# Two-part masked attention feeding a gated FFN on one core: products of zeros on TensorE in the opening, another order of opening loads and x pieces, a second batch masked by TensorE, and softmax pairs seven slots apart

## The chip, the core and the metric

The program runs on one core of a Trainium2 chip. The metric is the device time of one launch in microseconds, taken as the median of several runs. TensorE (PE in the profile, its weight loads PEld) does the matrix products, VectorE (DVE), ScalarE (ACT) and GpSimd (POOL) do elementwise work, and SyncE (SP) issues the DMAs. TensorE's clock has two levels, 1.2 and 2.4 GHz; the profile shows the granted one as a share of full speed.

## The reference

```python
# q, k, v: 8 batches, 8 heads, 576 positions, 64 wide
scores = scale * np.matmul(q, k.transpose(0, 1, 3, 2))
mask_local = (rel >= 0) & (rel < 32)                              # heads 0..3
mask_strided = (rel >= 0) & (pos[None, :] % 32 == pos[:, None] % 32)  # heads 4..7
scores = np.where(masks[None], scores, -1000000000.0)
attn = softmax(scores); attn_out = np.matmul(attn, v)
x = attn_out as (4608 tokens, 512)
h = x @ w_in                                                      # 512 -> 2048
g = h * (1.0 / (1.0 + np.exp(-1.702 * h)))
return g @ w_out                                                  # 2048 -> 512
```

## The kernel before

**Three stages.** The opening does the attention of batch 0 and prepares the first two weight blocks. Then eight passes, one for each batch, multiply x by w_in; each pass has eight weight blocks (`FP`), and during a pass the attention of the next batch is done beside the products. The results go to DRAM (`hid`). The last stage, from about 539 us, reads them back, applies the gate and multiplies by w_out; the change does not touch it.

**Products.** Each block of weights against one batch of x is done as seven products of half-size pieces (`product(n, k)`, k from 0 to 6, with sums and differences of quarters on both sides) instead of eight. Every number is split into a high part and a rest, so a product is six matmuls of 128x128 by 128x288. `combine(n, k)` takes the results out of PSUM: ACT copies for k = 0 and 2, DVE adds for the others.

**Slots.** The passes are written as a list of slots, one product each on average: block n begins at slot 7n and issues product k at slot 7n + 2k, so that two blocks interleave; a pass is 56 slots. In each slot first come the product and its combine, then whatever `side(slot, ...)` has put there, in the order of registration. All engines keep this program order until the last stage, so an instruction that waits holds everything behind it on its engine.

**Pairs.** The attention of a batch is six pairs (`PAIRS`), three local ones (96 queries in three windows) and three strided ones (128 rows). A pair goes through `scores` (TensorE, into the two banks `s_banks`), `masked` (DVE), `maxima` (DVE), `below` (POOL, subtracts the maximum), `exps` (ACT), `totals` (DVE), `scaled` (POOL), `turn` (four transposes on TensorE into `s_banks[0]`, an ACT copy) and `values` (TensorE into both `s_banks`, copied by ACT into the quarters of x, `xr`). For the six pairs of batch 0 (`p < PAIRS`, line 210) TensorE adds the mask itself: a product of the mask with an identity starts each bank and the scores are added to it; then `masked` takes the maximum out of PSUM and subtracts it, on DVE, and `maxima` and `below` aren't called. In a pass for batch b the pairs of batch b + 1 stand eight slots apart (seven in the first pass), line 558, with offsets 0, 1, 2, 3, 5, 6 for the six softmax steps and 11 and 14 for `turn` and `values`.

**x pieces.** From the quarters `11`, `12`, `21`, `22` four sums are made (`x_sum(1)`, `x_sum(2)` on DVE, `x_sum(3)`, `x_sum(4)` on POOL), in place where they can be. `x_high(k)` (ACT) and `x_low(k)` (DVE) split piece k into `xv[k]`, which product k reads. Since `values` of the next batch overwrites the quarters, its copies wait until `x_low` has read them. Lines 550 to 555 place these steps around the border between two passes (`at` is the first slot of the pass).

**Weights.** For each block of w_in, `w_scale` and `w_low` (ACT), `w_join` (DVE) put the numbers together from words, `w_sums` (POOL, four subtractions) makes the sums, `w_high` (ACT) and `w_rest` (DVE) split them, three quarters first (`sums` False) and four sums after (`sums` True). Blocks 0 and 1 are made in the opening, 2 to 7 in the first pass by `weigh` (line 567).

**The opening.** Lines 474 to 486 issue the loads; the loop at 489 runs nine steps, each with the scores of pair i, the transposes of pair i - 2, the values of pair i - 3, and the softmax steps; lines 527 to 539 prepare x pieces and block 1 before the first pass starts. Arena tiles hold most buffers and are reused: `mid[0]`, which the change also uses, is first written by a combine.

Of the kernel before, what the change touches and what calls it, by code (L numbers as in the profile page):

```python
# [30 lines left out]
FP = DFF // (2 * P)  # L31
PAIRS = 6
QL, KL = 96, 128
WL = 64
# [34 lines left out]
def attn_ffn(ctx, tc, qk, vs, weights, masks, ident, out):  # L69
# [84 lines left out]
    warm = const.tile([P, 1], F32, name="warm")  # L154
    vector.memset(warm, 0.0)
    scalar.activation(warm, warm, AF.Exp)
    for x in prs:
# [47 lines left out]
    def scores(p, banks):  # L205
# [3 lines left out]
        t = qks[p]  # L209
        onto = p < PAIRS  # L210
        if onto:
# [38 lines left out]
    def masked(p, banks):  # L250
        nq, nk, mask, pr, heads, srcs, (nmax, _, _) = parts_of(p, banks)
        if p < PAIRS:
            by = nmax[:nq].rearrange("p (i j) -> p i j", j=2)
            for j in range(2):
                vector.tensor_reduce(
                    out=by[:, :, j], in_=srcs[j], axis=AX.X, op=ALU.max, negate=True
                )
            for j in range(2):
                vector.tensor_tensor(
                    out=pr[:nq, :, j, :nk], in0=srcs[j], in1=over(by[:, :, j], 4, nk), op=ALU.add  # L260
                )
            return
# [16 lines left out]
    def exps(p, banks):  # L279
        heads = parts_of(p, banks)[4]  # L280
        scalar.activation(heads, heads, AF.Exp, scale=SCALE if p < PAIRS else 1.0)

# [18 lines left out]

    def values(p, banks):

# [21 lines left out]
        for u in range(U):  # L325
            src = banks[u][:, : 2 * n0].rearrange("p (g n) -> p g n", g=2)
            if kind == "l":
                h, o = divmod(c + u, 3)
                scalar.copy(out=x[("11", "21")[h]][:, :, o * QL : (o + 1) * QL], in_=src)
                continue  # L330
            n, r0, half = RES[c], R0[c + u], NPOS // 2
            src = src.rearrange("p g (r t) -> p g t r", r=n)
            for k, h in enumerate(("12", "22")):
                o = x[h].rearrange("p g (t r) -> p g t r", r=STRIDE)[:, :, :, r0 : r0 + n]
                scalar.copy(out=o, in_=src[:, :, k * half : (k + 1) * half])

# [15 lines left out]
    def x_sum(k):  # L352
# [3 lines left out]
        elif k == 2:  # L356
            vector.tensor_tensor(out=xr["11"], in0=xr["s1"], in1=xr["11"], op=ALU.subtract)
        elif k == 3:
# [27 lines left out]

    def w_sums(raw):
        f = raw.bitcast(F32)
        b11, b21, b22, b12 = (f[:, q, :, 1] for q in range(4))
        t1, t2, t3, t4 = (f[:, q, :, 0] for q in range(4))  # L390
        for o, x, y in ((t1, b12, b11), (t2, b22, t1), (t3, b22, b12), (t4, b21, t2)):
            gpsimd.tensor_tensor(out=o, in0=x, in1=y, op=ALU.subtract)
# [15 lines left out]

    def w_rest(i, raw, sums):
        src, hi, lo = w_part(i, raw, sums)  # L410
        vector.tensor_tensor(out=lo, in0=src, in1=hi.bitcast(F32), op=ALU.subtract)

# [66 lines left out]
    load_qk(2)  # L479
    load_v(1)  # L480
    load_w(0)
    for i in range(3, n0):
        load_qk(i)
        load_v(i - 1)
    load_v(n0 - 1)
    load_w(1)
    all_banks = [m_banks[i][x] for x in ("mx", "my", "mz") for i in range(2)]

    for i in range(n0 + 3):
        if i < n0:  # L490
            ss = all_banks[2 * (i % 2) : 2 * (i % 2) + 2]
# [3 lines left out]
        if 2 <= i <= n0 + 1:  # L495
            turn(i - 2, all_banks[4 + i % 2])
        if i >= 3:
            values(i - 3, s_banks)
            if i < 5:
                load_v(n0 + i - 3)  # L500
# [9 lines left out]
        if i == 4:  # L510
            w_join(raws[0])
            w_sums(raws[0])
            w_high(0, raws[0], False)
        if i == 5:
            w_rest(0, raws[0], False)
            w_high(0, raws[0], True)
        if i == 6:
            x_high(0)
            x_sum(3)
            w_rest(0, raws[0], True)  # L520
            x_low(0)
            w_scale(raws[1])
            w_low(raws[1])
        if i == 7:
            w_join(raws[1])
            w_sums(raws[1])
    load_w(2)
    x_sum(1)
    x_sum(2)
    for k in range(1, 7):  # L530
        x_high(k)
        x_low(k)
        if k == 2:
            x_sum(4)
            w_high(1, raws[1], False)
            w_rest(1, raws[1], False)
        if k == 4:
            w_high(1, raws[1], True)
            w_rest(1, raws[1], True)

# [7 lines left out]
    for b in range(B):  # L548
        at = b * PASS
        if b:  # L550
            for k, t in ((1, -9), (3, -8), (2, -5), (4, -1)):
                side(at + t, x_sum, k)
            for k, t in enumerate((-7, -4, -3, -1, 1, 3, 5)):
                side(at + t, x_high, k)
                side(at + t + (k < 6), x_low, k)
        for i in range(PAIRS if b + 1 < B else 0):
            p = (b + 1) * PAIRS + i
            s, t, t2 = (at - 9 + 8 * i, 11, 14) if b else (7 * i, 10, 12)
            side(s, scores, p, s_banks)
            side(s, load_qk, p + 2)  # L560
            for f, d in ((masked, 0), (maxima, 1), (below, 2), (exps, 3), (totals, 5), (scaled, 6)):
                side(s + d, f, p, s_banks)
# [4 lines left out]
    def weigh(i, at, then):  # L567
# [9 lines left out]
        for t, sums in ((0, False), (2, True)):  # L577
            later(then + t, w_high, i, sums)
            later(then + t + 1, w_rest, i, sums)

# [309 lines left out]
```

## Time and profile before

| | |
|---|---|
| median of 3 runs | 906.07 us (904.57 to 906.53) |
| profiled execution | 906.79 us, its span 904.8 us |
| granted clock, mean | 0.983 |
| PE busy | 851.1 us (94%) |
| DVE, ACT, POOL busy | 575.9, 418.8, 520.2 us |

The span runs from the first to the last instruction; the other 2.0 us of the profiled execution lie around it. Busy times are unions of an engine's instructions, and a busy PE is not a PE at its peak. The rows that matter are in the section further down: rows of stretches give the stretch and its length, then for each engine the busy time and the count of instructions, the granted clock and the DMA share; rows of the timeline give start, duration, engine, what was written from what, and in brackets the idle time before and what ended it.

### The profile page before, as it was taken

Reading aid. Unit: us, or ns where it says so; the run is one execution under the profiler, and the core shown is the slowest. Engines: PE = TensorE matmul, PEld = TensorE weight load, DVE = VectorE, ACT = ScalarE, POOL = GpSimd, SP = SyncE. Lnnn points to the kernel's source line nnn. Section 1 sums busy time; section 2 is a strip of 40 time slices with the busy share of each in tenths; the row PEclk is TensorE's granted clock in tenths of the full one; section 3 lists DMA queues with packets and bytes.
Section 4 is the critical chain, followed back from the end, with each engine's and each line's share of the span. In section 5 each row is a group of like instructions: output and inputs, shape, how many; then the busy total and the mean of one; then the engine's idle time right before and its main releaser. Section 6 shows DMA issues by size and latency. Waiting matters only on the chain.

```text
span 904.8 us, 23885 instructions
## 1 busy us (share of the span) xinstructions
PE 851.1 (94%) x9756; PEld 820.8 (91%) x9756; DVE 575.9 (64%) x941; ACT 418.8 (46%) x669; POOL 520.2 (57%) x497
## 2 busy tenths in 40 slices
PE   6689989989899899899899999999999999999997
PEld 4588879979899799799799999999999999999997
DVE  5798865655855755756656776665665566655663
ACT  3666533433433433434333655645554555445650
POOL 2667433423432432434331618999989998989990
PEclk9999999989999899999899999999999999999999
DMA  9358446647565557475556885344334434444331
GB/s 357 143 184 276 149 157 207 209 160 226 171 211 190 184 197 224 158 233 194 164 165 208 254 261 169 125 136 144 125 117 145 135 117 135 133 130 140 117 117 47
DMA packets 109644, 156.42 MB, mean 173 GB/s; under 512 B 9440, under 2 KB 87520, under 8 KB 108512
## 3 DMA queue, kind: packets, MB, share of 16 engines
q1 hardware_dynamic: 109536, 154.92, 52.8%
q8 instruction: 76, 1.25, 0.6%
q14 instruction: 32, 0.26, 0.1%
HBM read 100.35 MB, written 54.53 MB: 171 GB/s over the span
## 4 chain that ended last, share of the span: by engine, by line
PE 57%; DVE 15%; DMA 11%; issue 6%; ACT 5%; POOL 4%; SPq 2%; DVEq 0%; ACTq 0%; POOLq 0%
PE my L85 19%; PE mz L85 15%; PE mx L85 14%; PE s L85 10%; DMA arena<-hid 8%; DVE xa L85 6%; DVE arena L85 4%; POOL arena L85 3%; DVE ga L85 2%; ACT xa L85 2%; DMA hid<-arena 2%; SPq L85 2%; ACT arena L85 1%; POOL raw L85 1%; DMA early<-qk 1%
## 5 line engine op out<-in xcount | busy, mean ns | idle before, releaser
L85 POOL TENSOR_TENSOR arena<-arena 128x256 f32<-128x256 f32 (+1 forms) x304 | 354.4, 1183 | 118.5 <-ACT arena L85 46.6
L85 DVE TENSOR_TENSOR xa<-arena,xa 128x576 fp32r<-128x576 f32 (+1 forms) x104 | 171.4, 1657 | 70.9 <-ACT xa L85 68.5
L85 PE MATMUL my<-xa,w 128*128 128x288 f32 x1152 | 189.6, 308 | 5.3 <-DVE arena L85 4.2
L85 ACT ACTIVATE arena<-arena 128x1024 f32<-128x1024 f32 (+2 forms) x120 | 105.0, 876 | 174.0 <-DMA arena<-hid 149.0
L85 PEld LDWEIGHTS my<-xa,w 128*128 128x128 f32 x1152 | 166.9, 197 | 9.2 <-DVE arena L85 5.3
L85 DVE TENSOR_TENSOR arena<-mz,arena 128x288 f32<-128x288 f32 (+1 forms) x182 | 78.9, 442 | 88.4 <-PE mz L85 86.4
L85 PE MATMUL mx<-xa,w 128*128 128x288 f32 x768 | 129.1, 304 | 2.6 <-ACT arena L85 2.6
L85 PE MATMUL mz<-xa,w 128*128 128x288 f32 x768 | 130.5, 307 | 0.0
L85 ACT CAST xa<-arena 128x576 fp32r<-128x576 f32 (+1 forms) x104 | 118.2, 1140 | 21.0 <-DVE arena L85 11.0
L85 DVE TENSOR_TENSOR arena<-my,arena 128x288 f32<-128x288 f32 (+1 forms) x228 | 100.2, 444 | 40.8 <-PE my L85 40.0
L85 ACT COPY arena<-mx 128x288 f32<-128x288 f32 (+1 forms) x146 | 57.5, 394 | 142.5 <-PE mx L85 118.1
L85 POOL TENSOR_TENSOR arena<-arena,rinv 96x512 f32<-96x512 f32 (+1 forms) x48 | 52.3, 1091 | 114.8 <-DVE rinv L85 103.5
L85 PEld LDWEIGHTS mx<-xa,w 128*128 128x128 f32 x768 | 110.1, 192 | 4.6 <-ACT arena L85 3.0
L85 PEld LDWEIGHTS mz<-xa,w 128*128 128x128 f32 x768 | 112.5, 196 | 1.7 <-DVE arena L85 0.4
L85 POOL TENSOR_TENSOR arena<-arena,nmax 128x432 f32<-128x432 f32 (+1 forms) x42 | 48.9, 1165 | 101.4 <-DVE nmax L85 101.0
L85 ACT COPY arena<-s 128x90 f32<-128x90 f32 (+4 forms) x186 | 51.5, 339 | 110.5 <-PE s L85 91.8
L85 PEld LDWEIGHTS s<-arena 64*64 64x64 f32 (+2 forms) x3456 | 58.8, 133 | 39.5 <-ACT arena L85 26.6
L85 PE MATMUL s<-arena 64*64 64x32 f32 (+4 forms) x3456 | 70.6, 229 | 24.2 <-ACT arena L85 24.2
L85 PE MATMUL mx<-w_out,xa 128*128 128x256 f32 x576 | 84.0, 280 | 1.8 <-DVE xa L85 1.8
L85 PE MATMUL my<-w_out,xa 128*128 128x256 f32 x576 | 83.2, 280 | 0.0
L85 PE MATMUL mz<-w_out,xa 128*128 128x256 f32 x576 | 83.1, 280 | 0.0
L85 PEld LDWEIGHTS mx<-w_out,xa 128*128 128x128 f32 x576 | 74.6, 188 | 2.4 <-DVE xa L85 2.4
(62 smaller groups left out, 1049.3 us busy)
## 6 DMA issues: line engine op xcount, KB each, us to landing
hid<-arena SPq DMA_DIRECT2D x256, 144.0 KB, 2.6
arena<-hid SPq DMA_DIRECT2D x144, 256.0 KB, 3.3
arena<-qk SPq DMA_DIRECT2D x23, 448.0 KB, 4.1
arena<-qk SPq DMA_DIRECT2D x21, 472.0 KB, 3.8
out<-arena SPq DMA_DIRECT2D x36, 256.0 KB, 2.2
arena<-vs SPq DMA_DIRECT2D x23, 384.0 KB, 3.9
raw<-w_in SPq DMA_DIRECT2D x8, 1024.0 KB, 8.0
stage<-w_out SPq DMA_DIRECT2D x16, 512.0 KB, 4.9
```

Of the source, the lines that this page charges most:

```text
L85: ins = call(*args, **kw)
```

## The change

It has five parts.

1. `fill(n, bank)` issues n bf16 products of a zeroed tile (128x128 by 128x512) into a bank of PSUM that is unused at that time. In the steps of the opening loop 9, 3, 4, 1, 1, 1, 2, 3, 3 of them come first in TensorE's order, and 4 more before the first pass. DVE zeroes the tile (`mid[0]`).
2. The loads of pair 3's q and k and pair 2's v are issued before the first block of w_in instead of behind it. In the opening, the work on block 0 is spread over other steps (two of its sums go one step later), x piece 3 is prepared inside the loop, and the pieces left over follow in the order 2, 1, 5, 4, 6. In the loop's last step DVE copies the second bank of values. `x_sum(2)` is computed from `22` and `s3`.
3. `ONTO = 12` takes the place of `PAIRS` in the mask's conditions: batch 1's pairs are masked by TensorE too, without `maxima` and `below`, and `exps`, `totals`, `scaled` follow at offsets 2, 4, 5.
4. `w_rest` of the three quarters goes from DVE to POOL for block 0 and for blocks 2 to 7.
5. From the second pass on the pairs stand seven slots apart, the first three slots before the border; `exps`, `totals`, `scaled`, `turn`, `values` move to offsets 5, 6, 7, 10, 12. `x_sum`, `x_high` and `x_low` around the border get other slots.

```diff
+ONTO = 2 * PAIRS
...
+    zeros = mid[0].bitcast(BF16)[:, :512]
+    vector.memset(mid[0], 0.0)
...
-        onto = p < PAIRS
+        onto = p < ONTO
...
-        scalar.activation(heads, heads, AF.Exp, scale=SCALE if p < PAIRS else 1.0)
+        scalar.activation(heads, heads, AF.Exp, scale=SCALE if p < ONTO else 1.0)
...
+            copy = vector.tensor_copy if shared and u else scalar.copy
...
-            vector.tensor_tensor(out=xr["11"], in0=xr["s1"], in1=xr["11"], op=ALU.subtract)
+            vector.tensor_tensor(out=xr["11"], in0=xr["22"], in1=xr["s3"], op=ALU.subtract)
...
-    def w_rest(i, raw, sums):
+    def w_rest(i, raw, sums, engine=None):
         src, hi, lo = w_part(i, raw, sums)
-        vector.tensor_tensor(out=lo, in0=src, in1=hi.bitcast(F32), op=ALU.subtract)
+        (engine or vector).tensor_tensor(out=lo, in0=src, in1=hi.bitcast(F32), op=ALU.subtract)
...
+    load_qk(3)
+    load_v(2)
     load_w(0)
-    for i in range(3, n0):
+    for i in range(4, n0):
         load_qk(i)
         load_v(i - 1)
...
+    def fill(n, bank):
+
+        for _ in range(n):
+            matmul(bank, lhsT=zeros[:, :P], rhs=zeros, start=True, stop=True)
+
+    FILL = (9, 3, 4, 1, 1, 1, 2, 3, 3)
     for i in range(n0 + 3):
+        late = all_banks[4 + i % 2]
+        fill(FILL[i], late)
...
         if i == 4:
             w_join(raws[0])
-            w_sums(raws[0])
+            w_sums(raws[0], (0, 1))
+        if i == 5:
+            w_sums(raws[0], (2, 3))
             w_high(0, raws[0], False)
-        if i == 5:
-            w_rest(0, raws[0], False)
-            w_high(0, raws[0], True)
         if i == 6:
             x_high(0)
+            x_low(0)
             x_sum(3)
+            w_high(0, raws[0], True)
             w_rest(0, raws[0], True)
-            x_low(0)
+            w_rest(0, raws[0], False, gpsimd)
+        if i == 7:
+            x_high(3)
             w_scale(raws[1])
             w_low(raws[1])
-        if i == 7:
+            x_low(3)
             w_join(raws[1])
             w_sums(raws[1])
     load_w(2)
+    fill(4, all_banks[5])
+    x_high(2)
+    x_sum(2)
+    x_low(2)
+    x_high(1)
+    x_low(1)
     x_sum(1)
-    x_sum(2)
...
+    x_sum(4)
+    x_high(5)
+    w_high(1, raws[1], False)
+    x_low(5)
+    x_high(4)
+    x_low(4)
+    w_rest(1, raws[1], False)
+    w_high(1, raws[1], True)
+    x_high(6)
+    x_low(6)
+    w_rest(1, raws[1], True)
...
         if b:
-            for k, t in ((1, -9), (3, -8), (2, -5), (4, -1)):
-                side(at + t, x_sum, k)
-            for k, t in enumerate((-7, -4, -3, -1, 1, 3, 5)):
-                side(at + t, x_high, k)
-                side(at + t + (k < 6), x_low, k)
+            first = -8 if b == 1 else -11
+            side(at + first, x_sum, 1)
+            side(at + first + 1, x_sum, 3)
+            for k in range(7):
+                t = at + 2 * k - 6 + (k == 1)
+                side(t, x_high, k)
+                side(t + 1, x_low, k)
+            side(at - 4, x_sum, 2)
+            side(at, x_sum, 4)
...
-            s, t, t2 = (at - 9 + 8 * i, 11, 14) if b else (7 * i, 10, 12)
+            s, t, t2 = (at - 3 + 7 * i, 10, 12) if b else (7 * i, 10, 12)
             side(s, scores, p, s_banks)
             side(s, load_qk, p + 2)
-            for f, d in ((masked, 0), (maxima, 1), (below, 2), (exps, 3), (totals, 5), (scaled, 6)):
+            side(s, masked, p, s_banks)
+            if p < ONTO:
+                soft = ((exps, 2), (totals, 4), (scaled, 5))
+            else:
+                soft = ((maxima, 1), (below, 2), (exps, 5), (totals, 6), (scaled, 7))
+            for f, d in soft:
                 side(s + d, f, p, s_banks)
...
-            later(then + t + 1, w_rest, i, sums)
+            later(then + t + 1, w_rest, i, sums, *([] if sums else [gpsimd]))
```

## Rows read from the trace of the kernel before

**Rows 1.** Stretches, TensorE's products of x only: length, busy (count), clock, DMA, GB/s
```profile
48.20:113.00 64.80, 49.34 (x318) 1.00 0.66 212
...
429.40:491.30 61.90, 50.37 (x337) 0.94 0.55 177
```

**Rows 2.** The same view, two of the five stretches between borders
```profile
126.10:181.20 55.10, 47.04 (x322) 1.00 0.61 197
...
378.70:434.60 55.90, 48.20 (x330) 1.00 0.65 212
```

**Rows 3.** Waits of TensorE, 112 to 500 us: total, times, longest
```profile
PE s L85 <- ACT arena L85: 21.8, 6, 4.3
```

**Rows 4.** Timeline around the third of six borders
```profile
238.40 0.96 PE L85 MATMUL mz<-xa,w 128*128 128x288 f32 x6
...
241.34 1.36 POOL L85 TENSOR_TENSOR arena<-arena,nmax 96x512 f32<-96x512 f32 x1 [1.35 <-DVE nmax L85]
...
244.70 0.67 DVE L85 TENSOR_REDUCE ssum<-arena 96x8 f32<-96x512 f32 x1
...
246.15 1.54 DVE L85 TENSOR_TENSOR xa<-arena,xa 128x576 fp32r<-128x576 f32 x1
...
247.78 0.71 ACT L85 COPY arena<-s 128x108 f32<-128x108 f32 x4 [2.98 <-DVE xa L85]
...
248.23 1.08 PE L85 MATMUL s<-arena 64*64 64x54 f32 x32 [2.55 <-ACT arena L85]
...
249.24 1.81 PE L85 MATMUL mz<-xa,w 128*128 128x288 f32 x6
```

**Rows 5.** Stretches around two borders: PE, PEld, DVE, ACT, POOL, clock, DMA, GB/s
```profile
246.00:254.00 8.00, 5.77 (x58) 5.55 (x59) 4.61 (x9) 1.34 (x6) 1.96 (x2) 0.79 0.67 205
308.00:318.00 10.00, 6.16 (x56) 6.04 (x57) 6.00 (x14) 1.28 (x6) 4.48 (x6) 0.66 0.39 119
```

**Rows 6.** Timeline of the opening, TensorE alone
```profile
4.33 0.66 PE L85 MATMUL mx<-masks_sb 96*96 96x256 bf16 x2 [4.33 <-DMA masks_sb<-masks]
...
14.13 1.12 PE L85 MATMUL my<-early 64*64 64x54 f32 x32 [1.49 <-DMA early<-qk]
...
17.92 1.12 PE L85 MATMUL mx<-early 64*64 64x54 f32 x32
...
27.92 1.11 PE L85 MATMUL mz<-ident_sb,arena 128*128 128x128 f32 x4 [2.14 <-POOL arena L85]
...
34.24 1.33 PE L85 MATMUL s<-arena,early 54*64 54x54 f32 x32 [1.87 <-ACT arena L85]
...
48.20 1.81 PE L85 MATMUL my<-xa,w 128*128 128x288 f32 x6 [2.20 <-DVE arena L85]
```

**Rows 7.** Stretches of the opening, columns as in rows 5
```profile
14.00:26.00 12.00, 11.43 (x256) 9.32 (x256) 8.49 (x23) 6.56 (x13) 5.50 (x6) 1.00 1.03 401
...
36.10:48.20 12.10, 6.23 (x50) 4.76 (x48) 11.17 (x15) 7.80 (x12) 5.21 (x5) 1.00 0.36 127
```

**Rows 8.** Timeline of one weight block in the first pass
```profile
66.04 1.21 DVE L85 SCALAR_TENSOR_TENSOR raw<-raw 128x1024 uint32<-128x1024 uint32 x1
...
67.33 3.91 POOL L85 TENSOR_TENSOR raw<-raw 128x256 f32<-128x256 f32 x4 [3.03 <-DVE raw L85]
...
68.81 1.14 DVE L85 TENSOR_TENSOR w<-raw,w 128x768 fp32r<-128x768 f32 x1
...
72.08 1.04 POOL L85 TENSOR_TENSOR arena<-arena,nmax 96x512 f32<-96x512 f32 x1
...
72.43 1.77 DVE L85 TENSOR_TENSOR w<-raw,w 128x1024 fp32r<-128x1024 f32 x1 [0.86 <-ACT w L85]
...
74.86 1.21 DVE L85 SCALAR_TENSOR_TENSOR raw<-raw 128x1024 uint32<-128x1024 uint32 x1
```

**Rows 9.** Timeline late in the first pass: a transpose's wait, a POOL subtraction
```profile
98.72 0.55 PE L85 MATMUL s<-ident_sb,arena 96*128 96x96 f32 x4 [1.25 <-POOL arena L85]
...
103.16 1.44 POOL L85 TENSOR_TENSOR arena<-arena 128x576 f32<-128x576 f32 x1 [4.50 <-DVE arena L85]
```

More of the change, by code (lines that the diff above doesn't have):

```diff
@@ L251, in masked @@
         nq, nk, mask, pr, heads, srcs, (nmax, _, _) = parts_of(p, banks)
-        if p < PAIRS:
+        if p < ONTO:
             by = nmax[:nq].rearrange("p (i j) -> p i j", j=2)
@@ L300, in turn, with values @@
         scalar.copy(out=pts[p % 2][:, : 4 * nq], in_=bank[:, : 4 * nq])
-    def values(p, banks):
+    def values(p, banks, shared=False):
         kind, b, c = pairs[p]
@@ L326, in values @@
             src = banks[u][:, : 2 * n0].rearrange("p (g n) -> p g n", g=2)
+            copy = vector.tensor_copy if shared and u else scalar.copy
             if kind == "l":
                 h, o = divmod(c + u, 3)
-                scalar.copy(out=x[("11", "21")[h]][:, :, o * QL : (o + 1) * QL], in_=src)
+                copy(out=x[("11", "21")[h]][:, :, o * QL : (o + 1) * QL], in_=src)
                 continue
@@ L334, in values @@
                 o = x[h].rearrange("p g (t r) -> p g t r", r=STRIDE)[:, :, :, r0 : r0 + n]
-                scalar.copy(out=o, in_=src[:, :, k * half : (k + 1) * half])
+                copy(out=o, in_=src[:, :, k * half : (k + 1) * half])
     def x_from(k):
@@ L385, in w_join, with w_sums @@
         )
-    def w_sums(raw):
+    def w_sums(raw, some=range(4)):
         f = raw.bitcast(F32)
@@ L390, in w_sums @@
         t1, t2, t3, t4 = (f[:, q, :, 0] for q in range(4))
-        for o, x, y in ((t1, b12, b11), (t2, b22, t1), (t3, b22, b12), (t4, b21, t2)):
+        ops = ((t1, b12, b11), (t2, b22, t1), (t3, b22, b12), (t4, b21, t2))
+        for k in some:
+            o, x, y = ops[k]
             gpsimd.tensor_tensor(out=o, in0=x, in1=y, op=ALU.subtract)
@@ L495, in attn_ffn @@
         if 2 <= i <= n0 + 1:
-            turn(i - 2, all_banks[4 + i % 2])
+            turn(i - 2, late)
         if i >= 3:
-            values(i - 3, s_banks)
+            values(i - 3, s_banks, i == n0 + 2)
             if i < 5:
@@ L527, in attn_ffn @@
     load_w(2)
-    x_sum(1)
-    x_sum(2)
[L530 to L539, printed above, removed]
+    fill(4, all_banks[5])
[4 more added lines that the diff above has]
+    x_low(1)
+    x_sum(1)
+    x_sum(4)
[9 more added lines that the diff above has]
+    w_rest(1, raws[1], True)
     xr["s3"] = xr["21"]
@@ L550, in attn_ffn @@
         if b:
-            for k, t in ((1, -9), (3, -8), (2, -5), (4, -1)):
-                side(at + t, x_sum, k)
-            for k, t in enumerate((-7, -4, -3, -1, 1, 3, 5)):
-                side(at + t, x_high, k)
-                side(at + t + (k < 6), x_low, k)
+            first = -8 if b == 1 else -11
[7 more added lines that the diff above has]
+            side(at, x_sum, 4)
         for i in range(PAIRS if b + 1 < B else 0):
             p = (b + 1) * PAIRS + i
-            s, t, t2 = (at - 9 + 8 * i, 11, 14) if b else (7 * i, 10, 12)
+            s, t, t2 = (at - 3 + 7 * i, 10, 12) if b else (7 * i, 10, 12)
             side(s, scores, p, s_banks)
             side(s, load_qk, p + 2)
-            for f, d in ((masked, 0), (maxima, 1), (below, 2), (exps, 3), (totals, 5), (scaled, 6)):
+            side(s, masked, p, s_banks)
+            if p < ONTO:
+                soft = ((exps, 2), (totals, 4), (scaled, 5))
+            else:
+                soft = ((maxima, 1), (below, 2), (exps, 5), (totals, 6), (scaled, 7))
+            for f, d in soft:
                 side(s + d, f, p, s_banks)
```

## The prediction

> **What bounds the kernel now.** I began with the stretches. Between the borders of passes TensorE is the bound: of the 55.10 us from 126.10 it makes 322 product matmuls, one per 0.1711 us; in the last such stretch one per 0.1694 [rows 2]. A pass is 56 products of six, 336 matmuls, so at the mean rate, 0.1702, an undisturbed pass takes 57.2 us. The six passes from 113.0 to 491.3 took 378.3 us [rows 1], against 6 x 57.2 = 343.2: 35.1 us too many.
>
> The list of waits says where 21.8 of these lie: six waits of TensorE for an ACT copy, one at each border [rows 3]. The timeline of one border gives the chain behind it [rows 4]. POOL's `below` of the second pair sits there until 242.70, ACT's `exps` is queued behind it and with it `x_high(5)` and `x_high(6)`; DVE runs `totals` at 244.70, then the last two `x_low`, which end at 247.69; only then may ACT copy the values over the quarters (247.78), and the next scores find a bank at 248.23, after 2.55 us idle. The rest is the clock. A product that took 0.96 before the wait takes 1.81 after it [rows 4], and the granted clock of the stretch is 0.79 over 8 us, which is (1 - 0.79) x 2 x 8 = 3.4 us at 1.2 GHz; at the next border it is 0.66 over 10 us, 6.8 us at the low level [rows 5]. The six borders alternate between these two. So 35.1 - 21.8 = 13.3 us is work at the low level.
>
> The first pass is different. From 48.20 to 113.0 it makes 318 product matmuls, which at 0.1702 would be 54.1 us and took 64.8 [rows 1]. Weight preparation paces it: `w_join` starts at 66.04 and, one block later, at 74.86, a round of 8.82 us [rows 8], where seven slots need 57.2 / 8 = 7.15. The round is `w_join` (1.21), POOL's four sums (3.91, ending 71.24), ACT's `w_high`, DVE's last `w_rest` (72.43 to 74.20), two adds, the next `w_join`.
>
> The opening goes from one wait to the next: a load until 14.13, POOL at 27.92, ACT at 34.24, DVE at 48.20 [rows 6]. The clock column shows 1.00 there, but I don't take it at its word: six matmuls took 1.81 at 48.20 [rows 6], just what they took inside the border's stretch of 0.79 [rows 4]. From 14 to 26 TensorE is busy 11.43 of 12 us [rows 7] and stays at that level; its work there is half-array products and transposes.
>
> **The change, part by part.**
>
> *Borders.* Before, `exps` stood one slot behind `below` and two `x_high` behind that. Now `exps` is three slots behind `below`, a slot being 57.2 / 56 = 1.02 us, so 3.1 us, which covers its 1.36 [rows 4]. The last `x_low` stands at slot 7 of the pass, the first pair's `values` at slot 9 and the scores that need the bank at 11. The second pair's `exps`, also at 9, is registered behind those copies. So the wait for the copies should go, and with no stop of that length I expect the clock to stay. What is late next is DVE: from 5 slots before the border to 8 after it has seven `x_low` of 0.77 (half of the 1.54 for two), one `x_sum` that I put at the same size, ten adds and nine operations of softmax, which at the mean of DVE's instructions there (4.61 / 9 = 0.51 [rows 5], an upper value for them) are 9.7 us: 15.9 in all for fourteen slots, or 14.3 us. It ends up to 1.6 us behind, and one to two slots are in hand. I leave 0.5 us for each border, 3 us, and 0.5 for `scaled` held up by the w_out sums. Gain 35.1 - 3.5 = 31.6. The bounds: all 35.1, or 14 if half the waits stay at a length after which the clock falls. I take the upper part because the queue that held ACT is taken apart, not only shortened.
>
> *First pass.* `maxima` and `below` leave for the second batch: the 1.04 us on POOL at 72.08 [rows 8] goes, and DVE's four smaller operations replace three of the same total. `w_rest` of the quarters leaves DVE. At 68.81 it ran beside POOL's sums [rows 8]: four sums took 3.91; without it I expect 3.2, a gain of 0.7. But on POOL it now stands between `scaled` and the next sums. Its cost there is not shown; the nearest row is a subtraction of 576 columns in 1.44 [rows 9], so 768 columns take 1.92 alone, and by the sums (0.98 for 256 [rows 8]) 2.9; I take 2.2, nearer the plain one. What follows is the last `w_rest` on DVE. At 72.43 it took 1.77, and ended 1.08 after the POOL operation at 72.08 was over [rows 8]: it waited for that operation. In the new order POOL has `scaled` (about 0.95) and then 2.2 us of `w_rest`, together 3.15 from the end of the sums, where before it had 0.95 and 1.04 minus overlap, 1.88 (71.24 to 73.12). So DVE's `w_rest` ends 1.3 us later and with it the next `w_join`: +1.3 - 0.7 = +0.6 a round, and +0.8 with the extra operations of `masked` in front. Five rounds lie between the six joins: +4 us. If DVE gets through before POOL's long operation starts, the round is shorter by 0.5, or -2.5 in all; with 2.9 us on POOL it is +6 or a little over. The mask products add two bf16 matmuls for each pair, 0.59 us at the low clock (4.33 to 4.92, the first scores) [rows 6], about 0.3 at the high one; they lie in TensorE's idle time, which is 8.82 - 7.15 = 1.7 a round, and would cost 6 x 0.3 = 1.8 without it.
>
> The Trainium skill, page "SBUF — State Buffer", section "Who interferes with whom", says that a DVE instruction with two SBUF inputs and a GpSimd instruction that reads SBUF exclude each other, and that whichever starts first holds the other off for its whole length. By that rule the first pass gains nothing from moving work to POOL and comes out 4 us longer, as above; were the two merely independent, it would be 2.5 us shorter. The rows agree with the rule (1.08 us left after POOL ended), and I go by them.
>
> *Opening.* Nine products of zeros of 512 columns: a mask product of 256 columns takes about 0.22 at the low level (0.66 to the end of two, 0.43 for one), so 512 take 0.43 and nine 3.9 us, from about 1.2 to 5.1, where the first mask product stood at 4.33 [rows 6]: +0.8. Pair 3's load comes earlier by the 1 MB of w_in that it was behind, about 2.5 us at the 401 GB/s of that time [rows 7], but the transposes before it are held up by DVE, so I keep 0.5 of the 1.49. Steps 3, 4 and 5 are 17.92 - 14.13 = 3.8 us each, TensorE's own work. If the zeros raise the clock, the step falls to about 2.9 with its filler: -0.9 x 3 = -2.7; if not, +0.43 x 3 = +1.3. Two sums fewer stand before pair 4's `scaled`: -1.9 of the 2.14. The wait of 1.87 goes in part to the later copies: -1. Of DVE's 11.17 us from 36.10 [rows 7] one `x_low` moves ahead: -0.8. POOL's `w_rest`, 2.2, is new between `x_sum(3)` and the sums of block 1: +1.5. Together +0.8 - 0.5 - 2.7 - 1.9 - 1 - 0.8 + 1.5 = -4.6 with the clock, -0.6 without; I take -4. Bounds: -9 (no part of POOL's or the filler's cost shows) and +1.
>
> *Late part.* From 491 us the program is the same but for `x_low(6)` two slots later before a load into its place; I cost it at 0, hidden by eight slots until that load is used, and at 1 us at most otherwise.
>
> **Sum.** 906.8 - 31.6 + 4 - 4 = 875.2 for the profiled execution, which lies 0.7 above the median of the runs; so 874.5, say 875 for the median.
>
> **Rivals.**
> 1. *The stop moves.* DVE is 2 us late at the border, the copies with it, and TensorE stops for 2 us six times, some with a fallen clock (half of 13.3). For it: the 15.9 us against 14.3. Against it: at the third border DVE was hardly behind, it waited for ACT. Time: 875 + 12 - 3.5 + 6.6 = 890.
> 2. *Zeros don't wake the clock* or it falls again in the steps with one filler: the opening gives -0.6 and more stalls: 880. For it: 11.43 busy of 12 without a rise [rows 7].
> 3. *The change doesn't do what it says at the borders*: another wait holds ACT as long as before. 906.8 - 4 + 4 = 907. Against it: the release chain is explicit in the order.
> 4. *Slower.* Pairs at seven slots leave three slots from `scaled` to `turn` instead of five, and two from `turn` to `values` instead of three. If the softmax runs that late, TensorE stops at the transposes of each of the 36 later pairs, as it did for 1.25 at 98.72 in the first pass, where the pairs were seven apart already [rows 9]. 36 x 1.25 = 45: 920. It decides from 31.6 / 36 = 0.9 us a pair. Against it: this row is the only such wait over 1 us in that pass, and later POOL has little to do.
> 5. *Better*: the round in the first pass shrinks and the opening gains its 9: 875 - 6.5 - 5 = 863.
>
> **How the numbers follow.** Forecast 0.50; rival 1 0.17, rival 2 0.14, rival 3 0.05, rival 4 0.07, rival 5 0.07. The likeliest case has its own range, 866 to 884, from the 3.5 us at the borders, -2.5 to +6 in the first pass and +1 to -9 in the opening. The range for all, 862 to 893, takes in rivals 1, 2 and 5 and leaves out 3 and 4 and the tail of 1. A measurement of this kernel can tell 0.2%, 1.8 us, from no change. Faster 0.88, the same 0.05 (rival 3), slower 0.07.
>
> **What would show it.** Borders: no wait of TensorE for an ACT copy over 1 us from 112 to 500, granted clock 1.00 throughout, six passes in 344 to 348 us. First pass: `w_join` to `w_join` 9.4 to 9.7 with the last `w_rest` held by POOL's; 8.3 or less would prove that step wrong. Opening: a clock record well before 54 us, steps 3 to 5 in 3 us, the third k of block 0 near 44 rather than 48.20. The forecast is wrong if the stops at the borders survive with other names, or if waits at the transposes fill the passes.

## The result and the profile after

The changed kernel takes 874.66 us (874.5 to 876.07), 0.9666 of the time before, with a 95% interval of 0.9649 to 0.9683 (the kernel before had 905.39 in that measurement, 906.07 in the earlier one); the forecast was 875. Its profiled span is 872.7 us against 904.8. Run a second time among the experiments it took 874.45 us against 906.49, ratio 0.9643 (0.9622 to 0.9665).

The first view is the products of x by pass, as in [rows 1] and [rows 2]: stretch, length, TensorE's busy time and count, granted clock, DMA share, GB/s. Shown are the first pass, the first of the six after it and the last of them.

```profile
45.10:108.40 63.30, 48.28 (x319) 0.97 0.63 212
108.40:166.90 58.50, 49.11 (x338) 1.00 0.65 206
...
401.50:459.30 57.80, 48.96 (x339) 1.00 0.61 192
```

The six passes after the first end at 459.3 and take 350.9 us where they took 378.3: 27.4 us of the 32.1 by which the span fell. The stretch from the fourth product to the end of the first pass is 63.3 us against 64.8 [rows 1], 1.5 us. The fourth product starts at 45.09 instead of 48.20 [rows 6], 3.1 us. From the end of the last of these passes to the end of the span it is 413.5 us in one (904.8 - 491.3) and 413.4 in the other. The four add up to 32.1.

In the six passes (108 to 459 us) the list of TensorE's waits (total, times, longest) has one entry, another one than in [rows 3]. Over the 112 to 500 us of [rows 3] there is a second, which lies behind the six passes, in the one without pairs:

```profile
PE s L86 <- POOL arena L86: 5.7, 6, 1.4
PE my L86 <- DVE arena L86: 3.5, 4, 1.8
```

Five of the six waits last 0.9 to 1.4 us, one 0.3.

The timeline of the border that answers to [rows 4] shows it. The second pair's `below` comes at 232.68, the last `x_low` at 232.83 without a wait, and `exps` only at 234.85, behind the copies of the values (234.28). The copies wait only for the values themselves there. The place that is late is one step earlier: `x_low(4)` at 228.33 and `totals` behind it (229.07), so `scaled` on POOL runs at 230.42 and the four transposes wait 1.37 us.

```profile
228.33 0.82 DVE L86 TENSOR_TENSOR xa<-arena,xa 128x576 fp32r<-128x576 f32 x1
...
229.07 0.59 DVE L86 TENSOR_REDUCE ssum<-arena 128x8 f32<-128x432 f32 x1
...
230.42 0.91 POOL L86 TENSOR_TENSOR arena<-arena,rinv 128x432 f32<-128x432 f32 x1 [0.41 <-DVE rinv L86]
...
231.39 0.66 PE L86 MATMUL s<-ident_sb,arena 128*128 128x128 f32 x4 [1.37 <-POOL arena L86]
...
232.68 1.79 POOL L86 TENSOR_TENSOR arena<-arena,nmax 96x512 f32<-96x512 f32 x1 [1.35 <-DVE nmax L86]
232.83 0.74 DVE L86 TENSOR_TENSOR xa<-arena,xa 128x576 fp32r<-128x576 f32 x1
...
234.28 0.71 ACT L86 COPY arena<-s 128x108 f32<-128x108 f32 x4 [1.61 <-PE s L86]
234.85 0.65 ACT L86 ACTIVATE arena<-arena 96x512 f32<-96x512 f32 x1
```

The stretch around it, with the columns of [rows 5], shows DVE full, 7.93 of 8 us, and the clock up:

```profile
226.00:234.00 8.00, 6.63 (x115) 5.83 (x117) 7.93 (x17) 2.64 (x5) 6.08 (x7) 1.00 0.56 189
```

One weight block of the first pass, against [rows 8]: `w_join` at 53.88 and again at 62.93, 9.05 us. POOL's four sums take 3.18 instead of 3.91; then come `scaled` and POOL's new `w_rest`, 1.89 us, and DVE's last `w_rest` takes 2.73 because it stands until that one ends at 61.19.

```profile
53.88 1.21 DVE L86 SCALAR_TENSOR_TENSOR raw<-raw 128x1024 uint32<-128x1024 uint32 x1
...
55.17 3.18 POOL L86 TENSOR_TENSOR raw<-raw 128x256 f32<-128x256 f32 x4 [3.02 <-DVE raw L86]
...
58.30 1.05 POOL L86 TENSOR_TENSOR arena<-arena,rinv 96x512 f32<-96x512 f32 x1
...
59.30 1.89 POOL L86 TENSOR_TENSOR w<-raw,w 128x768 fp32r<-128x768 f32 x1
...
59.55 2.73 DVE L86 TENSOR_TENSOR w<-raw,w 128x1024 fp32r<-128x1024 f32 x1 [0.70 <-ACT w L86]
...
62.93 1.21 DVE L86 SCALAR_TENSOR_TENSOR raw<-raw 128x1024 uint32<-128x1024 uint32 x1
```

In the opening the nine products of zeros end at 4.67, and the clock is up from there: two mask products take 0.39 us where they took 0.66 [rows 6]. The pairs' steps follow at 4.52, 6.16, 8.01 and 11.51. From 34.7 to 48.3 the clock is down again, and the fourth product waits 2.36 us for DVE where it waited 2.20 [rows 6]. The last line is a stretch, with the columns of [rows 5]:

```profile
1.25 3.42 PE L86 MATMUL mz<-arena 128*128 128x512 bf16 x9 [1.25 <-DVE arena L86]
4.52 0.39 PE L86 MATMUL mx<-masks_sb 96*96 96x256 bf16 x2
...
11.51 0.35 PE L86 MATMUL my<-masks_sb 128*128 128x216 bf16 x2
...
45.09 1.81 PE L86 MATMUL my<-xa,w 128*128 128x288 f32 x6 [2.36 <-DVE arena L86]
...
34.70:48.30 13.60, 7.19 (x25) 6.13 (x26) 12.92 (x18) 8.39 (x12) 6.82 (x7) 0.50 0.35 125
```

### The profile page after: what moved, and what is told of

Its sections match the earlier page's. It is cut to its first block, busy times and chain, and to the rows that moved or that the text cites. A ratio compares the mean times of both kernels' runs of the same rounds, so it can differ in the third digit from the quotient of the medians.

```text
span 872.7 us, 23938 instructions
## 1 busy us (share of the span) xinstructions
PE 836.3 (96%) x9792; PEld 805.0 (92%) x9799; DVE 576.4 (66%) x943; ACT 422.0 (48%) x667; POOL 515.4 (59%) x498
## 5 line engine op out<-in xcount | busy, mean ns | idle before, releaser
L86 PE MATMUL my<-xa,w 128*128 128x288 f32 x1152 | 187.4, 302 | 8.6 <-DVE arena L86 6.2
L86 PEld LDWEIGHTS my<-xa,w 128*128 128x128 f32 x1152 | 163.0, 191 | 12.6 <-DVE arena L86 7.6
L86 PE MATMUL mx<-xa,w 128*128 128x288 f32 x768 | 125.3, 299 | 2.1 <-ACT arena L86 2.1
L86 POOL TENSOR_TENSOR arena<-arena,rinv 96x512 f32<-96x512 f32 (+1 forms) x48 | 48.4, 1007 | 132.2 <-DVE rinv L86 120.2
L86 DVE TENSOR_TENSOR arena<-mz,arena 128x288 f32<-128x288 f32 (+1 forms) x182 | 78.7, 440 | 58.4 <-PE mz L86 57.2
L86 PEld LDWEIGHTS mz<-xa,w 128*128 128x128 f32 x768 | 107.7, 189 | 3.1
L86 POOL TENSOR_TENSOR arena<-arena,nmax 128x432 f32<-128x432 f32 (+1 forms) x36 | 42.2, 1173 | 57.0 <-DVE nmax L86 55.5
L86 DVE TENSOR_TENSOR ga<-arena,ga 128x1792 fp32r<-128x1792 f32 x24 | 56.4, 2349 | 28.7 <-ACT ga L86 28.7
L86 PEld LDWEIGHTS mz<-w_out,xa 128*128 128x128 f32 x576 | 74.4, 188 | 0.0
```

The costliest lines, as they stand in the source:

```text
L86: ins = call(*args, **kw)
```

## The experiments

Each was timed in five rounds beside the kernel before on the same chip. Ratios are to the kernel before.

**Borders alone, in the kernel before.**

```diff
-            for k, t in ((1, -9), (3, -8), (2, -5), (4, -1)):
+            # x_sum, x_high, x_low, scores to values as in the changed kernel, for b >= 1
-            s, t, t2 = (at - 9 + 8 * i, 11, 14) if b else (7 * i, 10, 12)
+            s, t, t2 = (at - 3 + 7 * i, 10, 12) if b else (7 * i, 10, 12)
...
+            soft = ((exps, 5), (totals, 6), (scaled, 7)) if b else ((exps, 3), (totals, 5), (scaled, 6))
```

> The kernel before with the borders' part alone (pairs seven slots apart from three slots before the border, exps, totals, scaled, turn, values at 5, 6, 7, 10, 12, x pieces in the new slots); opening, masks and weight work as before. Theory S (the whole gain is the slots at the borders): the six ACT waits of 21.8 us go and the clock stays at 1.00 from 55 us on, six transposes wait about 1 us each as in the changed kernel, and the time falls by about 27 us to 877 to 880; opening and first pass stay as they were, product (0,3) at 48.2. Rival M (the moved mask and the opening are needed for it, since the first border inherits their lateness): the first border keeps a stop of over 2 us and the gain is 20 us or less.

Measured: 877.55 us, 0.967 (0.9644 to 0.9696). TensorE's waits at the borders are those of the changed kernel, 5.7 us in six transposes, and the six passes take 351.1 us. So this part is worth 28.6 us (906.11 - 877.55), where the whole change took off 30.7 and, the second time, 32.0. Opening, masks and weight work together are worth about 3 us between the medians, and since the intervals overlap these times can't tell that from nothing.

This run also has the old masks and the old weight work in the first pass. Its stretch from the fourth product (47.95) to the end of that pass is 63.35 us, against 64.80 in the kernel before [rows 1] and 63.30 in the changed one; in the run with the grid alone, further down, it is 63.00. The line counts TensorE's products of x only, as in [rows 1].

```profile
47.95:111.30 63.35, 48.31 (x319) 0.97 0.64 207
```

**Exps early again, in the changed kernel.**

```diff
-                soft = ((maxima, 1), (below, 2), (exps, 5), (totals, 6), (scaled, 7))
+                soft = ((maxima, 1), (below, 2), (exps, 3), (totals, 5), (scaled, 6))
```

> The changed kernel with exps, totals and scaled of the later pairs back at offsets 3, 5, 6. Theory Q (the stop came from exps queued close behind POOL's below on ACT): the ACT waits at the borders come back with 1.5 to 2.5 us each and the clock falls after some, 885 to 900 us. Theory D (the stop came from the last x_low standing in the slot of the values that overwrite its source; the distance of two slots is what cures it): no ACT wait over 1 us returns, the transposes wait less because scaled is a slot earlier, 870 to 875 us.

Measured: 877.7 us, 0.9681 (0.9656 to 0.9706). One wait for an ACT copy of 1.1 us came back, no more (112 to 480 us):

```profile
PE s L86 <- DVE arena L86: 5.2, 5, 1.4
PE s L86 <- ACT arena L86: 1.1, 1, 1.1
```

Theory Q, which was the prediction's reason, falls for the changed kernel: there the stops stay away without the three slots between `below` and `exps`. The time is above the 870 to 875 that theory D gave; the transposes wait as long as before, now for DVE's `masked` of the next pair.

**X pieces two slots later, in the changed kernel.** At the last border a load of the last stage overwrites the buffer of piece 6 before the late step has read it, so that border is not counted.

```diff
-                t = at + 2 * k - 6 + (k == 1)
+                t = at + 2 * k - 4 + (k == 1)
...
-            side(at - 4, x_sum, 2)
-            side(at, x_sum, 4)
+            side(at - 2, x_sum, 2)
+            side(at + 2, x_sum, 4)
```

> The changed kernel with every x_high, x_low, x_sum(2) and x_sum(4) at the borders two slots later, so that the last x_low stands in the slot of the first values again; exps stay at 5. Theory D (distance from the last x_low to values): the ACT waits at the borders come back, 1 to 3 us each, the clock falls at some, 884 to 900 us. Theory Q (exps behind below): none comes back, since exps is still three slots behind below; 874 to 877 us.

Measured: 885.48 us, 0.9765 (0.974 to 0.979). The time is one that theory D allowed, but not by its mechanism. No wait for an ACT copy was over 0.4 us. Products wait 0.89 to 0.99 us for `x_low` itself at each of the other borders, and 4.38 us at the last. Theory D falls as well: neither suspect alone brings the stop back.

**Without the products of zeros.**

```diff
-        fill(FILL[i], late)
...
-    fill(4, all_banks[5])
```

> The changed kernel without the 31 products of zeros. Theory Z (they raise the clock, and the opening gains by it): the clock record stays without an entry until about 50 us, steps 3 to 5 take TensorE 3.6 to 3.8 us each instead of about 3.4, product (0,3) starts 1.5 to 3 us later than 45.09, and the time is 2 to 3 us longer. Rival N (the opening is held by DVE, ACT, POOL and loads): product (0,3) within 0.7 us of 45.09 and the time within 1 us of the changed kernel's.

Measured: 875.48 us, 0.9655 (0.9631 to 0.9679): no difference from the changed kernel that these runs can tell. Product (0,3) started at 46.64, 1.55 later than in the first profile of the changed kernel; by theory Z that was the price of leaving them out. But the variants above, which have the zeros, had it at 47.03 and 47.20. So the first profile was looked at again:

**The changed kernel once more, unchanged.**

> The changed kernel once more, unchanged, since its profile had the clock up from 3.9 to 34.7 us in the opening, while two variants with the same opening had it up only from 6.4 or 6.9 to 13 us. Theory P (where the clock rises in the opening differs from execution to execution): the entries of the clock in the opening differ from those of the first profile, and product (0,3) falls anywhere from 45 to 47.3. Rival F (the products of zeros fix it): up before 5 us, product (0,3) at 45.1 within 0.3.

Measured: 874.45 us. Theory P holds: product (0,3) started at 47.16. The granted clock (after the five busy times) is 0.75 over the first 34 us in this profile, with 17 us at the low level while TensorE was busy 17.00 of 17.00; in the first profile it was 1.00:

```profile
0.00:34.00 34.00, 30.36 (x553) 19.89 (x554) 20.18 (x49) 17.77 (x38) 15.02 (x19) 0.75 0.74 287
11.40:28.40 17.00, 17.00 (x305) 12.19 (x305) 9.88 (x29) 9.43 (x22) 8.72 (x10) 0.50 0.92 367
```

```profile
0.00:34.00 34.00, 23.26 (x576) 15.65 (x587) 22.88 (x52) 18.49 (x39) 15.83 (x20) 1.00 0.74 287
```

This is the same program with two courses of the clock, 2.1 us apart at product (0,3) and 0.9 apart in span (873.6 and 872.7). The two profiles stay 2.1 us apart as far as the late pass, whose wait of 494.21 in the first comes at 496.40 in the second; there the first profile's clock fell for 3.4 us and the second's did not. The zeros raise the clock early in both, but do not hold it. Without them it also rose at about 8 us in this one profile and in that of the borders alone, and was down from 11 to 52 us. Over the nine profiles of kernels with the zeros product (0,3) starts at 44.71 and 45.09 in two and at 47.03 to 47.60 in seven, against 46.64 without them. Against that one profile the zeros gained 1.6 and 1.9 us there in the two in which the clock held, or fell for only 3.4 us, and nothing in the others; by the times they gained nothing that these runs can tell.

**W_rest back on DVE, in the changed kernel.**

```diff
-            later(then + t + 1, w_rest, i, sums, *([] if sums else [gpsimd]))
+            later(then + t + 1, w_rest, i, sums, *[])
```

> The changed kernel with w_rest of the three quarters of blocks 2 to 7 back on DVE. Theory L (POOL's 1.9 us operation holds DVE's last w_rest off for its length): that w_rest falls from 2.6 to 2.8 us to 1.2 to 1.4, POOL's four sums grow from 3.2 to 3.9, and the round of the first pass goes from 9.0 to 8.6 to 8.7, first pass 1.5 to 2 us shorter, time 872 to 874. Rival R (POOL's help pays): round 9.3 or more and the time 2 us longer.

Measured: 872.99 us, 0.9629 (0.9606 to 0.9653). `w_join` to `w_join` is 8.52 us, DVE's last `w_rest` 1.23, the sums 3.89, as theory L had them; from product (0,3) to the end of the pass it is 61.2 us against 63.3.

```profile
55.53 1.23 DVE L86 SCALAR_TENSOR_TENSOR raw<-raw 128x1024 uint32<-128x1024 uint32 x1
56.84 3.89 POOL L86 TENSOR_TENSOR raw<-raw 128x256 f32<-128x256 f32 x4 [3.74 <-DVE raw L86]
...
61.94 1.23 DVE L86 TENSOR_TENSOR w<-raw,w 128x1024 fp32r<-128x1024 f32 x1 [0.16 <-ACT w L86]
...
64.05 1.23 DVE L86 SCALAR_TENSOR_TENSOR raw<-raw 128x1024 uint32<-128x1024 uint32 x1 [0.15 <-ACT raw L86]
```

So moving `w_rest` to POOL costs 0.5 us a round, about 2 us in that stretch of the profile; in the times the gain of 1.5 us lies inside the intervals.

**Batch 1's mask back on DVE, in the changed kernel.**

```diff
-ONTO = 2 * PAIRS
+ONTO = PAIRS
...
+            elif not b:
+                soft = ((maxima, 1), (below, 2), (exps, 3), (totals, 5), (scaled, 6))
```

> The changed kernel with batch 1's mask back on DVE (maxima and below in the first pass, exps, totals, scaled at 3, 5, 6). Theory L: below is one more POOL operation of 0.9 to 1.0 us in the queue between POOL's w_rest and the next sums, and exps waits for it on ACT; the round of the first pass grows from 9.0 to 9.4 to 10, time 877 to 880. Rival O (the mask's place is free in that round): round 9.0 to 9.2, time within 1 us of the changed kernel's.

Measured: 875.99 us, 0.9665 (0.9645 to 0.9685). The rounds take 8.91 to 9.56 us, and the stretch 64.2 us instead of 63.3. Beside POOL's `w_rest` the mask on TensorE is worth about 1 us, less than theory L said; in the times it can't be told from nothing. With `w_rest` on DVE it is worth about 2 in that stretch: 61.2 us with the mask on TensorE, as in the run before this one, and 63.0 to 63.4 with neither, as in the borders alone and the grid alone. Having both, the changed kernel has 63.3, so parts 3 and 4 of the change together move this stretch by nothing in these profiles.

**Both suspects undone, in the changed kernel** (the last border left as it is).

```diff
-                t = at + 2 * k - 6 + (k == 1)
+                t = at + 2 * k - (4 if b + 1 < B else 6) + (k == 1)
...
-                soft = ((maxima, 1), (below, 2), (exps, 5), (totals, 6), (scaled, 7))
+                soft = ((maxima, 1), (below, 2), (exps, 3), (totals, 5), (scaled, 6))
```

> The changed kernel with both suspects at the borders undone at once, for six of the seven borders: x pieces two slots later and exps, totals, scaled at 3, 5, 6; each alone left no stop of over 1.1 us. Theory B (it takes both: exps of the second pair ahead of the last x_high on ACT, and the last x_low in the slot of the values): stops of 1.5 to 3.5 us for an ACT copy return at the borders, the clock falls at some, 885 to 900 us. Rival G (neither matters, the seven-slot grid and the place of the first pair do): no stop over 1.5 us, 875 to 881 us.

Measured: 881.73 us, 0.9722 (0.9696 to 0.9748), and no stop over 1.4 us from 112 to 480 us:

```profile
PE my L86 <- DVE xa L86: 5.9, 11, 1.0
PE s L86 <- ACT arena L86: 1.8, 2, 1.4
```

The longer of the two ACT waits, at the fourth border, shows the chain that theory B means. `exps` waits for POOL's `below`; behind it come the last `x_high`, the last `x_low`, the values' copies, and the scores that need the bank:

```profile
299.35 0.63 ACT L86 ACTIVATE arena<-arena 96x512 f32<-96x512 f32 x1 [2.72 <-POOL arena L86]
299.89 0.66 ACT L86 CAST xa<-arena 128x576 fp32r<-128x576 f32 x1
...
300.65 0.76 DVE L86 TENSOR_TENSOR xa<-arena,xa 128x576 fp32r<-128x576 f32 x1 [1.92 <-ACT xa L86]
...
301.50 0.71 ACT L86 COPY arena<-s 128x108 f32<-128x108 f32 x4 [0.95 <-DVE xa L86]
301.95 0.99 PE L86 MATMUL s<-arena 64*64 64x54 f32 x32 [1.40 <-ACT arena L86]
```

Theory B falls too, except in small. The old order is only partly back here: `exps` is ahead of the last `x_high`, but `totals` stays behind the last `x_low`. What is left of the difference to the kernel before is the grid of pairs. The next two take it from the other side.

**Exps late, in the kernel before.**

```diff
-            for f, d in ((masked, 0), (maxima, 1), (below, 2), (exps, 3), (totals, 5), (scaled, 6)):
+            soft = ((exps, 5), (totals, 6), (scaled, 7)) if b else ((exps, 3), (totals, 5), (scaled, 6))
+            for f, d in ((masked, 0), (maxima, 1), (below, 2)) + soft:
```

> The kernel before with one thing changed: exps, totals, scaled of the later pairs at offsets 5, 6, 7 instead of 3, 5, 6; grid of eight slots and x pieces as before. Theory Q (as the prediction had it: exps of the second pair, waiting for POOL's below, holds the last x_high on ACT and, through totals, the last x_low on DVE): the ACT waits at the borders shrink to under 1.5 us each, most falls of the clock go, 882 to 888 us. Rival G (the place of the pairs relative to the border decides): stops of 2 to 4 us stay, 900 to 907 us.

Measured: 891.97 us, 0.9841 (0.9811 to 0.9871), between the two theories.

```profile
PE s L85 <- ACT arena L85: 10.6, 6, 2.7
```

In the old grid the three slots between `below` and `exps` take away half of the 21.8 us; the clock still falls at four borders. At the fourth border the chain is the one shown for the run before, in the same order, and `exps` still waits: `below` took 3.79 us there and not 1.36 as in [rows 4]. The stop was 2.67 us.

```profile
295.23 3.79 POOL L85 TENSOR_TENSOR arena<-arena,nmax 96x512 f32<-96x512 f32 x1 [1.35 <-DVE nmax L85]
...
299.05 0.63 ACT L85 ACTIVATE arena<-arena 96x512 f32<-96x512 f32 x1 [3.15 <-POOL arena L85]
```

**The grid alone, in the kernel before.**

```diff
-            s, t, t2 = (at - 9 + 8 * i, 11, 14) if b else (7 * i, 10, 12)
+            s, t, t2 = (at - 3 + 7 * i, 10, 12) if b else (7 * i, 10, 12)
```

> The kernel before with the grid alone: later pairs seven slots apart from three slots before the border, turn and values at 10 and 12; exps, totals, scaled at 3, 5, 6 and all x pieces in the old slots. Theory G (the grid puts the second pair's exps and totals behind the last x_high and x_low, and four slots between the last x_low and the first values): no ACT wait over 1.2 us at the borders, clock up throughout, 875 to 880 us, as with the whole borders' part. Rival X (the new x slots are needed too): stops of 1.5 us or more at several borders, 885 us or more.

Measured: 883.35 us, 0.9744 (0.9715 to 0.9772). No wait for an ACT copy is left, and the clock falls once from 112 to 500 us. The transposes wait instead, nearly twice as long as in the changed kernel:

```profile
PE s L85 <- DVE arena L85: 10.2, 6, 1.9
```

The timeline of the third border shows why the copies are free: the second pair's `exps` runs at 239.98 and its `totals` at 240.64, both behind the last `x_low` (237.42) and the values' copies only just behind `exps`. In the old grid `totals` ran ahead of the last `x_low` [rows 4].

```profile
236.95 0.63 PE L85 MATMUL s<-ident_sb,arena 128*128 128x128 f32 x4 [1.79 <-DVE arena L85]
...
237.42 0.74 DVE L85 TENSOR_TENSOR xa<-arena,xa 128x576 fp32r<-128x576 f32 x1
...
239.98 0.63 ACT L85 ACTIVATE arena<-arena 96x512 f32<-96x512 f32 x1 [1.77 <-POOL arena L85]
240.51 0.67 ACT L85 COPY arena<-s 128x108 f32<-128x108 f32 x4
240.64 0.68 DVE L85 TENSOR_REDUCE ssum<-arena 96x8 f32<-96x512 f32 x1 [0.60 <-ACT arena L85]
```

So the grid alone is worth 22 us (905.59 - 883.35) of the borders' 28.6; the new x slots and the later `exps` together add the other 6.

**Eight slots again, in the changed kernel.**

```diff
-            first = -8 if b == 1 else -11
-            side(at + first, x_sum, 1)
-            side(at + first + 1, x_sum, 3)
+            side(at - 6, x_sum, 1)
+            side(at - 5, x_sum, 3)
...
-            s, t, t2 = (at - 3 + 7 * i, 10, 12) if b else (7 * i, 10, 12)
+            s, t, t2 = (at - 3 + 8 * i, 10, 12) if b else (7 * i, 10, 12)
```

> The changed kernel with the later pairs eight slots apart again, but still from three slots before the border; since the last values come five slots later, x_sum(1) and x_sum(3) stand at 6 and 5 slots before the border. Theory G (the place of the first two pairs decides, not the distance of seven): no ACT wait over 1.2 us returns, 873 to 878 us. Rival 7 (the distance of seven matters): stops or product waits of over 1 us at the borders, 880 us or more.

Measured: 892.47 us, 0.9842 (0.9814 to 0.987). No ACT wait was over 1.2 us, but the six transposes wait 13.2 us in all, up to 2.4, and the clock falls at four borders. The time is that of rival 7 in the expectation, but the run does not say by itself whether the distance or the two late `x_sum` did it: with eight slots the last values leave no room for them earlier. Room ahead of the border for those two is a use of seven slots that fits these runs; they don't show that it is the only one.

**W_rest on DVE, and the first pair's turn one slot later.**

```diff
-            later(then + t + 1, w_rest, i, sums, *([] if sums else [gpsimd]))
+            later(then + t + 1, w_rest, i, sums, *[])
...
-            side(s + t, turn, p, s_banks[0])
+            side(s + t + (b > 0 and i == 0), turn, p, s_banks[0])
```

> The changed kernel with two edits: w_rest of blocks 2 to 7 on DVE, as in the run that took 872.99, and the transposes of the first pair after each border one slot later. Theory T (the six waits of 0.9 to 1.4 us at those transposes are DVE's lateness of about one slot, so one slot more hides them): the waits fall under 0.3 us, six passes shorter by 3 to 5 us, 868 to 870 us. Rival C (the ACT copy then stands only one slot ahead of values, and TensorE waits there instead): values or scores wait 0.3 to 0.8 us, 871 to 873 us.

Measured: 870.06 us, 0.9599 (0.9571 to 0.9626). The waits at the transposes fall from 5.7 to 1.4 us and the six passes from 350.9 to 347.4. With `w_rest` on DVE alone they were still 5.6, so this is the turn's doing. Theory T was nearly right; of the late pass's waits it had said nothing. Against the changed kernel's second run the gain of both edits is 4.4 us between medians that were taken apart, with intervals that touch (0.9626 and 0.9622).

```profile
PE s L86 <- POOL arena L86: 1.4, 4, 0.6
```

## Why the prediction was right, step by step

The forecast change was -31.6 us for the span and the measured one -32.1. That they lie within a microsecond is partly luck: the borders gave 4.2 us less than forecast and the opening 0.9 less, and the first pass came out 5.5 better. The main term and its sign were right.

**Borders: -31.6 forecast, -27.4 measured.** That the waits and the falls of the clock would go together was right: no wait for an ACT copy is left, and the clock stays up from 48.3 to 495 us. The residual was mis-sized: 3.5 us were left, 7.7 remain (350.9 against 6 x 57.2 = 343.2, and not 344 to 348), and 5.7 of them are one wait a border at the first pair's transposes. I had given DVE's lateness 0.5 us a border, and `scaled` 0.5 in all. DVE's lateness of up to 1.6 us, which I had worked out, was real (7.93 busy of 8 us), but it shows at the transposes by way of `totals` and `scaled`, not at the copies where I had looked for it; one slot more there takes 4.3 of the 5.7 away.

**The reason given for it was half right.** I said that the stop goes because `exps` stands three slots behind `below`. In the old grid that takes away 11.2 of 21.8 us; at one border `below` took 3.79 us there, and not the 1.36 that three slots were to cover. In the new grid it isn't needed for that (`exps` back at 3: one wait of 1.1 us). What takes the stop away whole is that the pairs begin three slots before the border, with `turn` and `values` at 10 and 12; the grid alone shows it. With it the second pair's `exps` and `totals` come after the last `x_high` and `x_low` on their engines, which the prediction had as an aside about the order of registration. In the six kernels with that order (the changed one, borders alone, `exps` early, x pieces late, eight slots, grid alone) one wait for an ACT copy over 1 us came, of 1.1. The order is not the whole of it, though. With both suspects undone `exps` stands ahead of the last `x_high` again, the same order as with `exps` late in the kernel before, and there came two stops, 1.8 us in all, against six, 10.6 in all. What else the grid does was not taken apart.

**First pass: +4 forecast, -1.5 measured.** The mechanism is shown: POOL's `w_rest` holds DVE's for its length, and without it the round is 8.5 instead of 9.0. The Trainium skill, page "SBUF — State Buffer", section "Who interferes with whom", has it so that the later of the two is blocked wholly; the trace agrees, DVE's operation taking 2.73 us beside POOL's 1.89 and 1.23 without it. Two sizes were off: POOL needs 1.89 us and not 2.2, and the added operations of `masked` lie beside the sums, where DVE was free, so the round shown grew by 0.2 and not by 0.8. At 9.05 us it lies between the 9.4 to 9.7 that I had named and the 8.3 that would have proved the step wrong. Five rounds make 45.0 us against 44.4.

A term was put at nothing without a reason as well: the moved pairs. In the kernel before, the later pairs' first two scores stood at slots 47 and 55 of this pass; now they stand at 53 and 60, so that one falls into the next pass. The borders alone and the grid alone, both with the old masks and weight work, have 63.35 and 63.00 us from the fourth product to the end of the pass against 64.80, and 18.9 us behind the last `w_join` against 20.5. So the -1.5 belongs to the moved pairs, and masks and weight work, forecast at +4, came to nothing: about -2 for the mask alone, and +2 for POOL's `w_rest` on top of it.

**Opening: -4 forecast, -3.1 in the first profile and -1.0 in the second.** Both lie inside the bounds given (-9 to +1) and between the two sums worked out, -4.6 with the clock and -0.6 without. Rival 2 was right as a state that happens: in all eight other profiles of kernels with the zeros the clock fell at 11.1 to 13.7 us, in the steps with one product of zeros each, for 3.4 to 17 us; in both profiles of the changed kernel it fell a second time, for 13.6 us around product (0,3). In seven of the nine profiles product (0,3) stands at 47.0 to 47.6, and in the four with the old opening at 47.95 to 48.72; so about -1, near the sum without the clock, is the common case, and the -3.1 of the first profile the rarer one.

**Late part: 0 forecast, 0 measured**, but not as quietly as I had it. The pass without pairs is 3.6 us longer than before, with waits of 0.5, 1.0 and 1.8 us for DVE, and the last stage 3.7 shorter. The whole from slot 392 on varied between 410.8 and 415.9 us over the profiles, without an edit there; what decides it stays open.

Of the other rivals, 1 and 4 appear in small, as the six waits at the transposes; 3 and 5 did not come.

## What to carry to other kernels

Where engines keep program order, look at which instruction stands ahead of which on the engine that waits: here moving a whole chain a few slots past the critical pieces took off 22 us, and easing the wait that the profile names 14. Count a step moved to an idle engine by what it holds off, not by that engine's share of busy time: here it took back what the moved mask had gained. And a gain in a stretch where the clock takes different courses needs more than one profile: here one of them showed 3 us for a part that times could not tell from nothing.

## What the runs showed of the hardware

The length of a single wait did not decide whether TensorE's clock fell. In the late pass it fell to 1.2 GHz after a wait of 1.78 us for DVE (494.21 in the first profile of the changed kernel) and stayed up after the same wait of 1.89 (496.40) in the second. In the run with eight slots it stayed up after 2.15 us at 365.30 and fell after 2.15 at 118.50. The two lines have the columns of [rows 5], first the first profile and then the second:

```profile
494.00:504.00 10.00, 9.79 (x62) 9.79 (x63) 7.37 (x13) 4.89 (x8) 3.77 (x4) 0.83 0.77 244
494.00:504.00 10.00, 8.12 (x61) 7.88 (x61) 7.85 (x13) 5.75 (x9) 4.51 (x4) 1.00 0.80 244
```

In the opening the clock fell and stayed down for 17 us with TensorE recorded busy all the time (17.00 of 17.00), doing half-array products, transposes and a few products of zeros. And the clock column can read 1.00 where the clock is low: it does so in the opening of the kernel before, where two mask products took 0.66 us and with the clock up 0.39.
